# Linear attention ahead of two expert layers: the query exponential moved behind the transposes, the key maximum read from PSUM, zero-padded key tails, and the order of instructions from a table of offsets

## The chip, the cores and the metric

The kernel runs on one core of a Trainium2 chip. The time is device microseconds from the first to the last instruction of one launch, with what lies around them; smaller is better. The two versions are compared by the medians of several runs.

## What is computed

The program has three parts, one after the other: a linear attention, a mixture of eight experts, and a dense two-layer network with a rational activation. The change lies in the attention alone:

```
q_s = exp(q - max over d);   q_s = q_s / (sum over d + 1e-9)
k_s = exp(k - max over s);   k_s = k_s / (sum over s + 1e-9)
kv  = einsum('bhsd,bhse->bhde', k_s, v)
out = einsum('bhsd,bhde->bhse', q_s, kv)        # then laid out as 4608 rows of 512
```

There are 8 batches, 8 heads, 576 positions and a head size of 64, all in float32. The expert part then needs the router's logits of every row (and a skip score) before it knows which rows go to which expert.

## The kernel before

Each batch is cut into a main part of 512 positions (128 partitions times J = 4) and a tail of 64; the tails of two batches share one tile of 128 partitions. The function `attention` defines one small closure for each step and registers it with `op` under a name, an engine, a guessed duration, the steps it depends on and the buffers that it takes. For one batch the steps are these.

- Keys. `load_k` and `tail_k` bring the data in; `km2` and `km1` (L224, L231, L232) take maxima on VectorE; `krow` turns them with TensorE into PSUM (tile `pf`, L237), `kmx` (L247) reduces them, and `kbt` spreads the maximum over all partitions, again into `pf`. `kbc` (L256) is a ScalarE copy of this into the SBUF tile `kb`. `ksub0` on VectorE and `ksub2` on GpSimd (both L262) and `kst` (L268, the tail) subtract `kb`; `kexp0`, `kexp2` and `kxt` (L272, L276) are the exponentials on ScalarE. GpSimd sums them (`su2` L281, `su1` L286 and L287).
- Queries. `qx` (L293) is the maximum of each row on VectorE. With QA = 3, five heads are subtracted on GpSimd (`qs`, L303) and exponentiated in place (L313), and for three heads ScalarE does both at once with a bias (`qn` L297 negates the maximum, `qe` L310). The tail has `qxt`, `qst`, `qet` (L317, L321, L324). `tt` (L376) turns the exponentials with TensorE into PSUM (`pq`), and `tcp` (L380) copies them to SBUF as `eqT`.
- Products. `kv0` to `kv3` (L333, and L334 for the tail, which contracts the 64 partitions of its batch alone) accumulate k_s and v; `psum`, `rk` and `kn` (L339 to L349) normalise; `kvt`, `kvc`, `kvw`, `kwc` (L356 to L370) multiply the result with the router's weights; `tx` (L388) makes rows and logits at once. `tr`, `tl` (L394, L395, L413) and `tn` (L405 or L407) divide by the query's sum: `tn` is on VectorE except for the parts named in ON_ACT = (2,), which go to ScalarE. `store` sends 512 rows out, and `fin` (L428) adds up the logits.

PSUM has one `pf` bank for `krow`, `kbt` and `kvt` in turn, and one each for `pkv`, `psm` and `pq`; `px` has two buffers of two banks.

The order is made by `plan` (L136): it keeps a clock for each engine, takes the step that could start earliest, and among those within SLACK of it the one with the smallest due time, which is batch times PERIOD less a weighted length of the work behind the step. The steps are emitted in this order, and each engine, and SP's queue of transfers, runs its own steps strictly in it.

Of the kernel before, what the change touches and what calls it, by code (L numbers as in the profile page):

```python
# [37 lines left out]
QA = 3  # L38
URGENCY = {"pe": 2.16, "dve": 1.78, "act": 2.64, "pool": 1.71, "dma": 0.59}
HOP = 930.0  # L40
ROUND = 1.5 * 2 ** 23
TB = 384
PERIOD = 11200.0
SLACK = 100.0
ON_ACT = (2,)
# [90 lines left out]
def plan(ops, period, slack, sem=210.0, dma=1300.0):  # L136
    done, tail, users = {}, {}, {}
    for key, o in ops.items():
        for d in o["deps"]:
            users.setdefault(d, []).append(key)  # L140
    for key in reversed(list(ops)):
        tail[key] = ops[key]["dur"] * URGENCY[ops[key]["eng"]] + max([tail[u] + HOP for u in users.get(key, [])], default=0.0)
    prio = {key: o["batch"] * period - tail[key] for key, o in ops.items()}
    free, left, holds, order = {}, dict(ops), {}, []
    while left:
        cand = {}
        for key, o in left.items():
            if any(d in left for d in o["deps"]):
                continue
            wait = dma if o["eng"] == "dma" else sem  # L150
            t = max([done[d] + (wait if ops[d]["eng"] != o["eng"] else 0.0) for d in o["deps"]], default=0.0)
            for pool, bufs in o["takes"]:
                h = holds.get(pool, [])
                if len(h) >= bufs:
                    if any(u in left for u in h[-bufs]):
                        t = None
                        break
                    t = max([t] + [done[u] + wait for u in h[-bufs]])
            if t is not None:
                cand.setdefault(o["eng"], []).append((max(t, free.get(o["eng"], 0.0)), prio[key], key))  # L160
        eng = min(cand, key=lambda e: min(cand[e]))
        t0 = min(cand[eng])[0]
        t, _, key = min((c for c in cand[eng] if c[0] <= t0 + slack), key=lambda c: c[1])
        o = left.pop(key)
        free[eng] = t + o["dur"]
        done[key] = t + o["dur"] + o["lag"]
        for pool, _ in o["takes"]:
            holds.setdefault(pool, []).append(o["holds"][pool])
        order.append((t, key))
    return order, max(done.values())  # L170


def attention(tc, q, k, v, w_gate, w_skip, ca, cb, ident, ones, wg, av, bv, ab, logits, xd, gd, R):
    nc = tc.nc
    with ExitStack() as st:
# [38 lines left out]
        def load_tail(nm, bp):  # L214
            t = tails.tile([P, H, D], F32, name=nm + "t")
# [10 lines left out]
        def km1(b, c):  # L226
            m2, kt, hs = T["m2", b], T["kt", b // 2], part(b, c)[0]
# [24 lines left out]
        def kbc(b, c):  # L252
            hs, rs = part(b, c)
            if c == 0:
                T["kb", b] = work.tile([P, H, D], F32, name="kb", bufs=2)
# [18 lines left out]
        def kxt(b, c):  # L274
            kt = T["kt", b // 2][half(b), part(b, c)[0]]
# [7 lines left out]
        def su1(b):  # L283
            e2, kt = T["e2", b], T["kt", b // 2]
# [10 lines left out]
        def qn(b):  # L295
            T["qn", b] = work.tile([P, QA, J], F32, name="qn")
            nc.gpsimd.tensor_scalar(out=T["qn", b], in0=T["qx", b][:, H - QA:], scalar1=-1.0, scalar2=None, op0=ALU.mult)  # L297

        def qs(b):
            if ("eq", b) not in T:  # L300
                T["eq", b] = work.tile([P, J, H, D], F32, name="eq", bufs=3)
            hs = slice(0, H - QA)
            nc.gpsimd.tensor_tensor(out=T["eq", b][:, :, hs].rearrange("p j h d -> p h j d"), in0=T["q", b][:, hs],  # L303
                                    in1=T["qx", b][:, hs].unsqueeze(3).to_broadcast([P, H - QA, J, D]), op=ALU.subtract)

        def qe(b, j):
            if ("eq", b) not in T:
                T["eq", b] = work.tile([P, J, H, D], F32, name="eq", bufs=3)
            for h in range(H - QA, H):
                nc.scalar.activation(T["eq", b][:, j, h], T["q", b][:, h, j], AF.Exp, bias=T["qn", b][:, h - H + QA, j:j + 1])  # L310
            if QA < H:
                eq = T["eq", b][:, j, 0:H - QA]
                nc.scalar.activation(eq, eq, AF.Exp)  # L313
# [9 lines left out]
        def qet(b):  # L323
            nc.scalar.activation(T["qt", b // 2], T["qt", b // 2], AF.Exp)  # L324

        def kv(b, r):
# [3 lines left out]
            ek, vm, kt, vt, pkv = T["ek", b], T["v", b], T["kt", bp], T["vt", bp], T["pkv", b]  # L330
# [3 lines left out]
            nc.tensor.matmul(out=pkv[:, r, :], lhsT=kt[half(b), hs, :], rhs=vt[half(b), hs, :], start=False, stop=True)  # L334
# [95 lines left out]
        for b in range(B):  # L430
# [5 lines left out]
            k_users = {"k": fc("ksub0") + fc("ksub2"), "v": [("kv3", b)], "q": [("qe3", b)]}  # L436
            for nm in "kvq":
# [3 lines left out]
                if not odd:  # L441
                    tu = {"k": [("kv3", bo), ("su1", bo)], "v": [("kv3", bo)], "q": [("tt4", bo)]}[nm]
                    op("tail_" + nm, b, DMA, 1500.0, [], lambda nm=nm, b=b: load_tail(nm, b // 2), takes=[(nm + "t", 3, tu)], lag=900.0)
            for c in cs:
# [4 lines left out]
                for n, eng, dur, deps, fn, takes in (  # L449
                        ("km2", DVE, 1135.0, [d("load_k")], lambda b=b, c=c: km2(b, c), first(("m2", 1, fc("km1")))),  # L450
                        ("km1", DVE, 1331.0, [d("km2"), ("tail_k", be)], lambda b=b, c=c: km1(b, c), first(("m1", 1, fc("krow")))),
                        ("krow", PE, 440.0, [d("km1")], lambda b=b, c=c: krow(b, c), [("pf", 1, [d("kmx")])]),
                        ("kmx", DVE, 600.0, [d("krow")], lambda b=b, c=c: kmx(b, c), []),
                        ("kbt", PE, 440.0, [d("kmx")], lambda b=b, c=c: kbt(b, c), [("pf", 1, [d("kbc")])]),
                        ("kbc", ACT, 480.0, [d("kbt")], lambda b=b, c=c: kbc(b, c), first(("kb", 2, fc("ksub2") + fc("ksub0") + fc("kst")))),
                        ("ksub0", DVE, 1150.0, [d("kbc")], lambda b=b, c=c: ksub(b, c, nc.vector, 0), first(("ek", 2, [("kv3", b), ("su2", b)]))),
                        ("kst", DVE, 600.0, [d("kbc")], lambda b=b, c=c: kst(b, c), []),
                        ("ksub2", POOL, 2303.0, [d("kbc"), ("ksub0c0", b)], lambda b=b, c=c: ksub(b, c, nc.gpsimd, 2), []),
                        ("kexp0", ACT, 950.0, [d("ksub0")], lambda b=b, c=c: kexp(b, c, 0), []),
                        ("kexp2", ACT, 950.0, [d("ksub2")], lambda b=b, c=c: kexp(b, c, 2), []),  # L460
                        ("kxt", ACT, 520.0, [d("kst")], lambda b=b, c=c: kxt(b, c), [])):
                    op(f"{n}c{c}", b, eng, dur * w + 70.0 * (len(cs) - 1), deps + pc(n), fn, takes=takes)
            op("su2", b, POOL, 2303.0, fc("kexp0") + fc("kexp2"), lambda b=b: su2(b), takes=[("e2", 1, [("su1", b)])])
            op("su1", b, POOL, 2552.0, [("su2", b)] + fc("kxt"), lambda b=b: su1(b), takes=[("e1", 2, [("psum", b)])])
# [766 lines left out]
```

## Time and profile before

| | us |
|---|---|
| median of 3 runs | 1425.42 |
| lowest and highest | 1420.71, 1426.38 |
| the profiled execution | 1417.86 |
| its span | 1416.2 |

In the views below a name such as L262 is a line of the kernel, `out<-in` are the program's tiles, a shape is partitions x elements, and an engine's "idle before" is put down to what ended it. PE is TensorE, DVE is VectorE, ACT is ScalarE, POOL is GpSimd, SPq is the queue that issues transfers.

### The profile page before, as it was taken

Reading aid. Unit: us, or ns where it says so; the run is one execution under the profiler, and the core shown is the slowest. Engines: PE = TensorE matmul, PEld = TensorE weight load, DVE = VectorE, ACT = ScalarE, POOL = GpSimd, SP = SyncE. Lnnn points to the kernel's source line nnn. Section 1 sums busy time; section 2 is a strip of 40 time slices with the busy share of each in tenths; the row PEclk is TensorE's granted clock in tenths of the full one; section 3 lists DMA queues with packets and bytes.
Section 4 is the critical chain, followed back from the end, with each engine's and each line's share of the span. In section 5 each row is a group of like instructions: output and inputs, shape, how many; then the busy total and the mean of one; then the engine's idle time right before and its main releaser. Section 6 shows DMA issues by size and latency. Waiting matters only on the chain.

```text
span 1416.2 us, 22263 instructions
## 1 busy us (share of the span) xinstructions
PE 1338.9 (95%) x7470; PEld 1206.2 (85%) x7470; DVE 1129.7 (80%) x2091; ACT 919.4 (65%) x1811; POOL 314.6 (22%) x252
## 2 busy tenths in 40 slices
PE   5888949999899999799999999999999999999998
PEld 4877939888789889688999999999999999999997
DVE  7799775657665655499988888888888888888887
ACT  2756713635342422499887878787778787878776
POOL 6655414556445443143000000000000000000000
PEclk9999969999999999899999999999999999999999
DMA  9885365566646574331010100000000000000000
GB/s 279 212 260 166 106 176 172 209 241 214 225 157 235 199 259 163 115 133 57 23 45 1 45 23 23 23 23 23 23 23 23 23 23 23 23 23 23 1 23 23
DMA packets 86928, 143.82 MB, mean 102 GB/s; under 512 B 21924, under 2 KB 52644, under 8 KB 85744
## 3 DMA queue, kind: packets, MB, share of 16 engines
q1 hardware_dynamic: 79696, 125.88, 27.1%
q0 software_dynamic: 7072, 16.06, 3.7%
q8 instruction: 70, 1.15, 0.3%
q14 instruction: 90, 0.74, 0.2%
HBM read 110.66 MB, written 35.15 MB: 103 GB/s over the span
## 4 chain that ended last, share of the span: by engine, by line
PE 54%; ACT 2%; DVE 2%; DMA 0%; issue 0%; ACTq 0%; SPq 0%
PE py L1168 26%; PE ph L1123 26%; PE pt L1107 1%; DVE gl L1149 0%; DMA wos<-wc_out 0%; DVE qq L1147 0%; ACT gh L1132 0%; ACT qq L1138 0%; DVE pn L1155 0%; ACT m L1136 0%; ACT pn L1140 0%; DVE qq L1153 0%; ACT r L1143 0%; DVE r L1151 0%; DVE pn L1157 0%
## 5 line engine op out<-in xcount | busy, mean ns | idle before, releaser
L1168 PE MATMUL py<-woh,gl 128*128 128x512 f32 x576 | 227.5, 395 | 0.2 <-DVE gl L1149 0.2
L1168 PE MATMUL py<-woh,gh 128*128 128x512 f32 x576 | 227.4, 395 | 0.0
L1168 PE MATMUL py<-wol,gh 128*128 128x512 f32 x576 | 226.9, 394 | 0.0
L1132 ACT CAST gh<-pn 128x384 fp32r<-128x384 f32 x192 | 98.8, 514 | 142.2 <-PE py L1168 137.0
L1149 DVE TENSOR_TENSOR gl<-pn,gh 128x384 fp32r<-128x384 f32 x192 | 110.0, 573 | 69.5 <-ACT gh L1132 69.5
L1138 ACT ACTIVATE qq<-m,ab 128x384 f32<-128x384 f32 x192 | 136.5, 711 | 6.4
L1123 PE MATMUL ph<-xh,wi0h 128*128 128x384 f32 x384 | 129.6, 338 | 0.3 <-DVE pn L1158 0.2
L1123 PE MATMUL ph<-xh,wi0l 128*128 128x384 f32 x384 | 129.6, 338 | 0.0
L1123 PE MATMUL ph<-xl,wi0h 128*128 128x384 f32 x384 | 129.0, 336 | 0.0
L1168 PEld LDWEIGHTS py<-woh,gl 128*128 128x128 f32 x576 | 108.0, 188 | 24.4 <-DVE gl L1149 1.2
L1140 ACT ACTIVATE pn<-ph,av 128x384 f32<-128x384 f32 x192 | 125.7, 655 | 0.0
L1158 DVE SCALAR_TENSOR_TENSOR pn<-pn,av,ph 128x384 f32<-128x384 f32 x192 | 118.1, 615 | 6.8
L1168 PEld LDWEIGHTS py<-wol,gh 128*128 128x128 f32 x576 | 108.2, 188 | 17.8
L1168 PEld LDWEIGHTS py<-woh,gh 128*128 128x128 f32 x576 | 108.3, 188 | 17.4 <-ACT gh L1132 0.5
L1153 DVE TENSOR_TENSOR qq<-m,qq 128x384 f32<-128x384 f32 x192 | 106.9, 557 | 17.9 <-ACT qq L1138 4.3
L830 PE MATMUL ph<-xth,w1h 128*128 128x256 f32 x416 | 119.1, 286 | 1.6 <-ACT cvs L760 0.7
L830 PE MATMUL ph<-xtl,w1h 128*128 128x256 f32 x416 | 118.8, 286 | 0.1
L830 PE MATMUL ph<-xth,w1l 128*128 128x256 f32 x416 | 118.6, 285 | 0.0
L1155 DVE SCALAR_TENSOR_TENSOR pn<-pn,av,r 128x384 f32<-128x384 f32 x192 | 117.4, 611 | 0.1
L1143 ACT ACTIVATE r<-qq,qc 128x384 f32<-128x384 f32 x192 | 116.0, 604 | 0.0
L1147 DVE SCALAR_TENSOR_TENSOR qq<-qq,r 128x384 f32<-128x384 f32 x192 | 108.7, 566 | 0.0
L1151 DVE SCALAR_TENSOR_TENSOR r<-qq,r 128x384 f32<-128x384 f32 x192 | 106.9, 557 | 0.0
(236 smaller groups left out, 3331.0 us busy)
## 6 DMA issues: line engine op xcount, KB each, us to landing
hold<-in_moe_w_dram SPq DMA_DIRECT2D x8, 2048.0 KB, 9.2
w2s<-in_moe_w_dram SPq DMA_DIRECT2D x8, 2048.0 KB, 10.1
hold<-xd SPq DMA_DIRECT2D x12, 768.0 KB, 4.3
out_dram<-o SPq DMA_DIRECT2D x36, 256.0 KB, 2.1
vm<-in_v_dram SPq DMA_DIRECT2D x8, 1024.0 KB, 9.3
qm<-in_q_dram SPq DMA_DIRECT2D x8, 1024.0 KB, 10.6
xd<-xs SPq DMA_DIRECT2D x8, 1024.0 KB, 5.3
raw<-in_moe_w_in_dram SPq DMA_DIRECT2D x16, 512.0 KB, 7.9
```

The lines of the kernel that those rows point to most:

```text
L830: nc.tensor.matmul(out=ph[:, u, :], lhsT=a[:, k, fs], rhs=b[:, k, :], start=(n == 0), stop=(n == 3 * KD - 1))
L1123: nc.tensor.matmul(out=ph, lhsT=w[:, k, :], rhs=x[:, k, :], start=(n == 0), stop=(n == 3 * KD - 1))
L1138: nc.scalar.activation(qq, m, AF.Identity, scale=ab[:, 1:2], bias=ab[:, 0:1])
L1140: nc.scalar.activation(pn, ph, AF.Identity, scale=av[:, 3:4], bias=av[:, 2:3])
L1143: nc.scalar.activation(r2, T[("q",) + second], AF.Ln, bias=qc)
L1147: nc.vector.scalar_tensor_tensor(out=q3, in0=q3, scalar=1.0 + 1e-6, in1=r3, op0=ALU.add, op1=ALU.mult)
L1149: GL(nc).tensor_tensor(out=gl, in0=pn4, in1=gh.bitcast(F32), op=ALU.subtract)
L1151: nc.vector.scalar_tensor_tensor(out=r3, in0=q3, scalar=2.0, in1=r3, op0=ALU.subtract, op1=ALU.mult, reverse0=True)
L1153: nc.vector.tensor_tensor(out=qq, in0=m, in1=qq, op=ALU.mult)
L1155: nc.vector.scalar_tensor_tensor(out=p3, in0=p3, scalar=av[:, 0:1], in1=r3, op0=ALU.add, op1=ALU.mult)
L1158: nc.vector.scalar_tensor_tensor(out=pn, in0=pn, scalar=av[:, 1:2], in1=ph, op0=ALU.add, op1=ALU.mult)
L1168: nc.tensor.matmul(out=py, lhsT=g[:, ts_], rhs=w[:, f, :], start=(f == 0 and n == 0), stop=(f == KF - 1 and n == 2))
```

## The change

- `tcp` becomes an exponential that reads PSUM; the transposes turn the differences q - max. `qn`, `qe`, `qet` go, and `qs` subtracts all eight heads on GpSimd, in two instructions of four heads.
- `kbc` and the tile `kb` go. `ksub0`, `ksub2` and `kst` read the spread maximum straight from `pf`; `ksub2` moves from GpSimd to VectorE. The bank stays taken until all three are done.
- The key tails lie in four fixed tiles, each with 64 partitions zeroed once by GpSimd at the start, and the tail's product contracts all 128 partitions. There are two pairs of tail buffers in place of three.
- `tn0` goes to ScalarE beside `tn2` (not for the last batch, as before).
- `plan` is replaced: every step has a moment, batch times PERIOD + OFFSET of its name + SHIFT of its batch, and the steps are emitted in the order of these moments, each as soon as what it depends on, and the users of the buffer that it takes, have been emitted.

```diff
-QA = 3
-PERIOD = 11200.0
-ON_ACT = (2,)
+PERIOD = 16040
+SHIFT = [-160, -440, -700, -1800, -2750, -2900, -3460, -4400]
+OFFSET = {
...
+    "kexp2c1": -23420, "qx1": -22210, "kstc0": -19620, "tail_v": -18620, "tx2": -18400, "su1": -15680, "km2": -14420, "load_v": -13390,
...
+ON_ACT = (0, 2)
...
+def plan(ops):
+    def at(key):
...
+        return b * PERIOD + OFFSET[name] + SHIFT[b]
...
+    while left:
+        key = next(k for k in left if ready(k))
...
+        for i in range(NKT):
+            t = keep.tile([P, H, D], F32, name=f"kt{i}")
+            nc.gpsimd.memset(t[64 * (1 - i % 2):64 * (1 - i % 2) + 64], 0.0)
...
-            nc.scalar.copy(T["kb", b][:, hs], T["pb", b, c][:, rs].rearrange("p r (h d) -> p (r h) d", h=2))
...
-                              in1=T["kb", b][:, hs].unsqueeze(2).to_broadcast([P, hs.stop - hs.start, 2, D]), op=ALU.subtract)
+                                    in1=kb(b, c).unsqueeze(2).to_broadcast([P, hs.stop - hs.start, 2, D]), op=ALU.subtract)
...
-            nc.tensor.matmul(out=pkv[:, r, :], lhsT=kt[half(b), hs, :], rhs=vt[half(b), hs, :], start=False, stop=True)
+            nc.tensor.matmul(out=pkv[:, r, :], lhsT=kt[:, hs, :], rhs=vt[:, hs, :], start=False, stop=True)
...
-            nc.scalar.copy(T["eqT", b, j], T["pq", b, j])
+            nc.scalar.activation(T["eqT", b, j], T["pq", b, j], AF.Exp)
...
-                        ("kbt", PE, 440.0, [d("kmx")], lambda b=b, c=c: kbt(b, c), [("pf", 1, [d("kbc")])]),
+                        ("kbt", PE, 440.0, [d("kmx")], lambda b=b, c=c: kbt(b, c), [("pf", 1, [d("ksub2"), d("kst")])]),
...
-                        ("ksub2", POOL, 2303.0, [d("kbc"), ("ksub0c0", b)], lambda b=b, c=c: ksub(b, c, nc.gpsimd, 2), []),
+                        ("ksub2", DVE, 1180.0, [d("kbt"), ("ksub0c0", b)], lambda b=b, c=c: ksub(b, c, 2), []),
```

Sorted by this table, GpSimd's queue repeats su2, su1, (qst,) qs0, qs1 of one batch. VectorE's queue, from the second half of the keys of batch 4 on, reads: ksub2.4 kn.3 km1.5 tr1.2 tl1.2 tn1.2 tr2.2 tl2.2 kmx.5 qx0.4 qx1.4 tr3.2 tl3.2 tn3.2 fin.2 ksub0.5 kst.5 tr0.3 tl0.3 rk.4 km2.6, then the tables, then ksub2.5 and so on (the number is the batch). SP's queue in the middle reads: load_k.5 store.0 tail_v.4 load_v.4 load_q.4 load_k.6 store.1 tail_q.4 store_tail.1 tail_k.6 load_v.5 load_q.5 load_k.7 store.2.

## Rows read from the trace of the kernel before

**Rows 1.** Stretch, length, busy PE, PEld, DVE, ACT, POOL, clock, DMA share, GB/s.

```profile
0.00:35.00 35.00, 18.34 (x68) 14.16 (x68) 26.89 (x30) 10.53 (x21) 22.61 (x30) 1.00 1.03 279
35.00:70.00 35.00, 31.75 (x220) 28.41 (x220) 27.66 (x43) 24.68 (x69) 23.82 (x14) 1.00 0.79 210
70.00:105.00 35.00, 28.09 (x212) 25.78 (x213) 34.20 (x57) 21.93 (x64) 20.79 (x27) 0.96 0.89 256
105.00:140.00 35.00, 29.97 (x209) 27.25 (x208) 34.15 (x68) 20.56 (x54) 20.60 (x11) 0.89 0.59 168
140.00:181.00 41.00, 37.82 (x305) 35.27 (x302) 32.32 (x94) 27.45 (x84) 14.29 (x14) 1.00 0.43 118
```

**Rows 2.** Timeline of VectorE at the end of the attention: start, us, instruction.

```profile
180.09 0.78 DVE L428 TENSOR_REDUCE logits<-lr 128x45 f32<-128x360 f32 x1
```

**Rows 3.** Timeline of SP's queue behind it.

```profile
191.15 2.13 SPq L787 DMA_DIRECT2D hold<-in_moe_w_dram  x4
```

**Rows 4.** VectorE's waits in the attention: us in total, times, longest.

```profile
DVE rq L394 <- PE px L388: 7.3, 10, 1.7
DVE m L224 <- DMA km<-in_k_dram: 5.6, 2, 4.1
```

**Rows 5.** VectorE's groups with each shape apart: busy us, mean ns.

```profile
L262 DVE TENSOR_TENSOR ek<-km,kb 128x1024 f32<-128x1024 f32 x7 | 15.4, 2193 | 1.9 <-ACT kb L256 1.9
L231 DVE TENSOR_TENSOR m<-m 128x512 f32<-128x512 f32 x7 | 13.7, 1962 | 0.1
L224 DVE TENSOR_TENSOR m<-km 128x1024 f32<-128x1024 f32 x7 | 11.9, 1693 | 0.1
L268 DVE TENSOR_TENSOR kt<-kt,kb 64x512 f32<-64x512 f32 x7 | 11.1, 1579 | 0.2
L232 DVE TENSOR_TENSOR m<-m,kt 64x512 f32<-64x512 f32 x7 | 9.9, 1412 | 0.2
L268 DVE TENSOR_TENSOR kt<-kt,kb 64x256 f32<-64x256 f32 x2 | 2.7, 1341 | 0.0
```

**Rows 6.** Single lines: duration in ns, least, median and most.

```profile
L293 DVE TENSOR_REDUCE qx<-qm x16: 1202/1208/1220, 19.9 to 152.6; 128x16 f32<-128x1024 f32 x16
L407 DVE TENSOR_TENSOR xs<-px,rq x25: 639/679/682, 53.3 to 177.7; 128x512 f32<-128x512 f32 x25
```

**Rows 7.** Timeline of all engines from 95 us on, VectorE and GpSimd alone.

```profile
95.09 5.95 DVE L231 TENSOR_TENSOR m<-m 128x512 f32<-128x512 f32 x1
...
95.66 2.33 POOL L303 TENSOR_TENSOR eq<-qm,qx 128x1280 f32<-128x1280 f32 x1
...
98.16 2.34 POOL L262 TENSOR_TENSOR ek<-km,kb 128x1024 f32<-128x1024 f32 x1
```

**Rows 8.** ScalarE's groups with each shape apart: busy us, mean ns, idle before.

```profile
L310 ACT ACTIVATE eq<-qm,qn 128x64 f32<-128x64 f32 x96 | 26.2, 338 | 2.2 <-POOL qn L297 2.1
L380 ACT COPY eqT<-pq 128x512 f32<-128x512 f32 x36 | 21.1, 586 | 22.3 <-PE pq L376 19.5 <-PE px L388 2.6
L313 ACT ACTIVATE eq<-eq 128x320 f32<-128x320 f32 x32 | 14.6, 457 | 0.0
L405 ACT ACTIVATE xs<-px,rq 128x64 f32<-128x64 f32 x56 | 12.3, 334 | 2.0 <-DVE lr L413 1.4 <-issue 0.5
L324 ACT ACTIVATE qt<-qt 128x512 f32<-128x512 f32 x4 | 2.5, 623 | 0.4 <-POOL qt L321 0.4
```

**Rows 9.** Timeline of TensorE around one tail product.

```profile
74.31 1.06 PE L333 MATMUL pkv<-vm,ek 128*128 128x128 f32 x8
75.29 0.49 PE L334 MATMUL pkv<-vt,kt 64*128 64x128 f32 x2
75.71 0.66 PE L237 MATMUL pf<-ident,m 128*128 128x128 f32 x4
```

**Rows 10.** Timeline of GpSimd: its first tensor operation.

```profile
10.60 1.71 POOL L262 TENSOR_TENSOR ek<-km,kb 128x512 f32<-128x512 f32 x1 [5.87 <-ACT kb L256]
```

**Rows 11.** The waits of SP's queue: us in total, times, longest.

```profile
SPq L417 <- DVE xs L407: 67.6, 6, 20.2
```

More of the change, by code (lines that the diff above doesn't have):

```diff
@@ L133, in tail_col @@
     return bp * (2 * J + 1) + 2 * J
[L136 to L144, printed above, removed]
-    while left:
[L146 to L170, printed above, removed]
@@ new lines, in plan, with ready @@
+def plan(ops):
+    def at(key):
+        name, b = key
+        if b and name.endswith("c0"):
+            name = name[:-2]
+        return b * PERIOD + OFFSET[name] + SHIFT[b]
+    left, holds, order = sorted(ops, key=at), {}, []
+    gone = set()
+    def ready(key):
+        o = ops[key]
+        if any(d not in gone for d in o["deps"]):
+            return False
+        return all(len(holds.get(p, [])) < n or all(u in gone for u in holds[p][-n]) for p, n in o["takes"])
+    while left:
+        key = next(k for k in left if ready(k))
+        left.remove(key)
+        gone.add(key)
+        for p, _ in ops[key]["takes"]:
+            holds.setdefault(p, []).append(ops[key]["holds"][p])
+        order.append(key)
+    return order
@@ L214, in load_tail @@
         def load_tail(nm, bp):
+            if nm == "k":
+                for i in range(2):
+                    b = 2 * bp + i
+                    nc.sync.dma_start(out=kts[b % NKT][64 * i:64 * i + 64], in_=k[b, :, MAIN:S, :].rearrange("h p d -> p h d"))
+                return
             t = tails.tile([P, H, D], F32, name=nm + "t")
@@ L250, in kbt, with kb, ksub @@
             T["pb", b, c] = rows(lambda r: T["mx", b][:, r:r + 1].to_broadcast([P, P]), part(b, c)[1])
[L252 to L255, printed above, removed]
-            nc.scalar.copy(T["kb", b][:, hs], T["pb", b, c][:, rs].rearrange("p r (h d) -> p (r h) d", h=2))
-        def ksub(b, c, eng, j0):
+        def kb(b, c):
+            return T["pb", b, c][:, part(b, c)[1]].rearrange("p r (h d) -> p (r h) d", h=2)
+        def ksub(b, c, j0):
             hs = part(b, c)[0]
@@ L274, in kxt @@
         def kxt(b, c):
-            kt = T["kt", b // 2][half(b), part(b, c)[0]]
+            kt = kts[b % NKT][half(b), part(b, c)[0]]
             nc.scalar.activation(kt, kt, AF.Exp)
@@ L293, in qx, with qs @@
             nc.vector.tensor_reduce(out=T["qx", b][:, hs], in_=T["q", b][:, hs], op=ALU.max, axis=AX.X)
[L295 to L313, printed above, removed]
+        def qs(b, h):
+            if h == 0:
+                T["qd", b] = work.tile([P, J, H, D], F32, name="qd", bufs=3)
+            hs = slice(4 * h, 4 * h + 4)
+            nc.gpsimd.tensor_tensor(out=T["qd", b][:, :, hs].rearrange("p j h d -> p h j d"), in0=T["q", b][:, hs],
+                                    in1=T["qx", b][:, hs].unsqueeze(3).to_broadcast([P, 4, J, D]), op=ALU.subtract)
         def qxt(b):
@@ L435, in attention @@
             fc = lambda n: [(f"{n}c{c}", b) for c in cs]
-            k_users = {"k": fc("ksub0") + fc("ksub2"), "v": [("kv3", b)], "q": [("qe3", b)]}
+            k_users = {"k": fc("ksub0") + fc("ksub2"), "v": [("kv3", b)], "q": [("qs1", b)]}
             for nm in "kvq":
@@ L449, in attention @@
                 for n, eng, dur, deps, fn, takes in (
-                        ("km2", DVE, 1135.0, [d("load_k")], lambda b=b, c=c: km2(b, c), first(("m2", 1, fc("km1")))),
-                        ("km1", DVE, 1331.0, [d("km2"), ("tail_k", be)], lambda b=b, c=c: km1(b, c), first(("m1", 1, fc("krow")))),
+                        ("km2", DVE, 1250.0, [d("load_k")], lambda b=b, c=c: km2(b, c), first(("m2", 1, fc("km1")))),
+                        ("km1", DVE, 1400.0, [d("km2"), ("tail_k", be)], lambda b=b, c=c: km1(b, c), first(("m1", 1, fc("krow")))),
@@ L457, in attention @@
[L457 to L461 removed]
+                        ("kmx", DVE, 700.0, [d("krow")], lambda b=b, c=c: kmx(b, c), []),
@@ new lines, in attention @@
+                        ("kbt", PE, 440.0, [d("kmx")], lambda b=b, c=c: kbt(b, c), [("pf", 1, [d("ksub2"), d("kst")])]),
+                        ("ksub0", DVE, 1180.0, [d("kbt")], lambda b=b, c=c: ksub(b, c, 0), first(("ek", 2, [("kv3", b), ("su2", b)]))),
+                        ("kst", DVE, 690.0, [d("kbt")], lambda b=b, c=c: kst(b, c), []),
+                        ("ksub2", DVE, 1180.0, [d("kbt"), ("ksub0c0", b)], lambda b=b, c=c: ksub(b, c, 2), []),
+                        ("kexp0", ACT, 1060.0, [d("ksub0")], lambda b=b, c=c: kexp(b, c, 0), []),
@@ L462, in attention @@
+                        ("kexp2", ACT, 1060.0, [d("ksub2")], lambda b=b, c=c: kexp(b, c, 2), []),
+                        ("kxt", ACT, 620.0, [d("kst")], lambda b=b, c=c: kxt(b, c), [])):
                     op(f"{n}c{c}", b, eng, dur * w + 70.0 * (len(cs) - 1), deps + pc(n), fn, takes=takes)
[L463 to L464 removed]
+            op("su2", b, POOL, 2400.0, fc("kexp0") + fc("kexp2"), lambda b=b: su2(b), takes=[("e2", 1, [("su1", b)])])
@@ L472, in attention @@
-            for j in range(J):
-                op(f"qe{j}", b, ACT, 240.0 * QA + (90.0 + 53.3 * (H - QA)) * (QA < H), [("qn", b), ("qs", b)] + [(f"qe{j - 1}", b)] * (j > 0), lambda b=b, j=j: qe(b, j),
-                   takes=eq_take if QA == H and j == 0 else [])
+                op(f"qx{h}", b, DVE, 1180.0, [("load_q", b)] + [("qx0", b)] * h, lambda b=b, h=h: qx(b, h), takes=[("qx", 2, [("qs1", b)])] if h == 0 else [])
+                op(f"qs{h}", b, POOL, 2130.0, [(f"qx{h}", b)] + [("qs0", b)] * h, lambda b=b, h=h: qs(b, h), takes=[("qd", 3, [("tt3", b)])] if h == 0 else [])
@@ L488, in attention @@
-            op("kwc", b, ACT, 180.0, [("kvw", b)], lambda b=b: kwc(b))
+            op("kvc", b, ACT, 600.0, [("kvt", b)], lambda b=b: kvc(b), takes=[("kvT", 1, [("kvw", b)])])
+            op("kvw", b, PE, 900.0, [("kvc", b)], lambda b=b: kvw(b), takes=[("psm", 1, [("kwc", b)])])
+            op("kwc", b, ACT, 370.0, [("kvw", b)], lambda b=b: kwc(b))
             for j in range(nj):
-                src = ("qet", b) if j == J else (f"qe{j}", b)
+                src = ("qst", b) if j == J else ("qs1", b)
@@ L496, in attention @@
-                op(f"tl{j}", b, DVE, 145.0, [(f"tr{j}", b)] + chain("tl"), lambda b=b, j=j: tl(b, j), takes=[("lr", 2, [("fin", b)])] if j == 0 else [])
-                op(f"tn{j}", b, ACT if j in ON_ACT and b < B - 1 else DVE, 1590.0 if j in ON_ACT and b < B - 1 else 605.0, [(f"tl{j}", b)] + chain("tn"), lambda b=b, j=j: tn(b, j),
+                op(f"tr{j}", b, DVE, 350.0, [(f"tx{j}", b)] + chain("tr"), lambda b=b, j=j: tr(b, j), takes=[("rq", 2, [(f"tn{i}", b) for i in range(nj)])] if j == 0 else [])
@@ L498, in attention @@
+                op(f"tl{j}", b, DVE, 220.0, [(f"tr{j}", b)] + chain("tl"), lambda b=b, j=j: tl(b, j), takes=[("lr", 2, [("fin", b)])] if j == 0 else [])
+                op(f"tn{j}", b, ACT if j in ON_ACT and b < B - 1 else DVE, 2650.0 if j in ON_ACT and b < B - 1 else 670.0, [(f"tl{j}", b)] + chain("tn"), lambda b=b, j=j: tn(b, j),
                    takes=[("xs", 2, [("store", b)])] if j == 0 else [("xt", 2, [("store_tail", b)])] if j == J else [])
@@ L518, in load_small @@
             nc.sync.dma_start(out=bv, in_=cb.unsqueeze(0).to_broadcast([P, 2]))
-        order, span = plan(ops, PERIOD, SLACK)
+        order = plan(ops)
         with tc.manual_schedule():
-            for _, key in order:
+            for key in order:
                 ops[key]["fn"]()
```

57 lines of the change are left out of this document (22 added, 35 removed), and 11 rows, old and new, of the table OFFSET.

## The prediction

> **What bounds the kernel now.** The chain of waits is of no help here: followed back from the end it stays in the last part of the program. So I read the stretches first. The attention ends at 180.87 us, where `fin` of the last batch has the last logits [rows 2]; the first expert weights are fetched 10 us later, because their number comes out of these logits [rows 3]. Nothing of the experts can begin before, so what the attention saves comes off the whole time one for one, and nothing else in the program is changed. In the table by stretch VectorE is the fullest engine: 34.20 and 34.15 of 35 us between 70 and 140, and 26.89 + 27.66 + 34.20 + 34.15 + 32.32 = 155.2 us of the 181 in all; ScalarE and GpSimd have room everywhere, and TensorE is full in the last stretch alone [rows 1]. VectorE's 25.8 idle us are mostly waits at the start, for the first keys (5.6), and for `tx` (7.3) [rows 4]. So the first question is what VectorE's 155.2 us consist of.
>
> Its groups answer that. A subtraction of 1024 elements takes 2.19 us, a maximum of 512 takes 1.96, a subtraction of 512 takes 1.58 [rows 5], yet a maximum over 1024 never takes more than 1.22 and a product of 512 that reads PSUM never more than 0.682 [rows 6]. The stretched ones all read two SBUF tiles. One of them shows how: L231 begins at 95.09 and ends at 101.04, and GpSimd runs two tensor operations in that time, the last of them done at 100.50 [rows 7]. While GpSimd works, a VectorE instruction with two SBUF operands stands still, and all of its queue with it; one with one SBUF operand, or with PSUM, does not.
>
> **The change part by part**, on VectorE first. Undisturbed prices are 1.21 us for 1024 elements and 0.68 for 512 [rows 6], half as much for half (0.6 and 0.4, my estimate).
>
> - `ksub0` and `kst` read their maximum from PSUM, so each keeps one SBUF operand and should no longer be held. `ksub0`: 15.4 - 7 x 1.21 = 6.9 us less. `kst`: 11.1 + 2.7 - 7 x 0.68 - 2 x 0.4 = 8.2 us less [rows 5]. Together 15.1. No row has a subtraction of an SBUF tile and a PSUM tile of this size; the nearest is L407, which reads PSUM beside SBUF and shows no hold in 25 cases, so I take all of it; the other bound is none of it.
> - `ksub2` comes from GpSimd: 7 x 1.21 + 2 x 0.68 = 9.8 us more.
> - `tn0` leaves for seven batches: 7 x 0.68 = 4.8 us less. On ScalarE it is eight instructions of 0.334 us each, 12.3 us for the seven if they cost what `tn2` costs [rows 8].
> - `km2` and `km1` keep two SBUF operands. Their holds are now 11.9 - 8.5 + 13.7 - 4.8 + 9.9 - 4.8 = 17.4 us [rows 5]. What becomes of them is a matter of the order. In the table's queue `km1` stands two places behind `ksub2`; GpSimd's next step, `su2`, needs the exponential of what `ksub2` just made, so GpSimd should be idle then. `km2` stands behind all of qx, tn3, fin, ksub0 and kst, when the train su2, su1, qs0, qs1 should be nearly through. I take two thirds as gone, 11.6 us; the bounds are all of it, and none.
> - Idle time stays at 25.8 us. New waits of VectorE for `kbt` and old ones for `tx` may trade places; I allow 8 us either way, which is about the whole of the second [rows 4].
>
> TensorE: 32 tail products contract 128 partitions. Before, a pair of tail instructions took 75.71 - 75.29 = 0.42 us from start to start, a pair of full ones 0.98 / 4 = 0.245 [rows 9]; 32 x 0.175 = 5.6 us less, worth nothing by itself while VectorE sets the pace. The zeroing is four small fills on GpSimd, whose first real work came only at 10.60 [rows 10], and now comes later still.
>
> ScalarE loses L310 and L313 (26.2 + 14.6 us), the copies `kbc` and the tail's exponential (2.5), and gains the 12.3 of `tn0`. An exponential of 128x512 takes 623 ns against 586 for the copy that it replaces [rows 8]: 36 x 0.04 = 1.3 us, hidden. ScalarE had more than 10 us of room in every stretch [rows 1], so none of that counts in the sum; it shortens the path from `qx` to `tx`, and that is why I let the idle time not grow.
>
> GpSimd loses `ksub2` and `qn` and gains three heads: 2.33 us for five [rows 7] makes 3.7 for eight. It ends below its 102 us [rows 1].
>
> Transfers: their number and size stay. In SP's queue each store now stands in front of the next loads of values and queries, and waits for `tn2` on ScalarE; the queue already spent 67.6 us behind stores without starving VectorE beyond the start [rows 4, 11]. With two pairs of key tails instead of three, `tail_k` waits for a batch further back; it is asked for more than a batch ahead, so I cost it at nothing. If the cover is gone, a late key load costs up to the longest such wait, 20.2 us, once.
>
> [...]
>
> **The sum.** 155.2 - 15.1 + 9.8 - 4.8 - 11.6 = 133.5 us busy, plus 25.8 idle, makes an attention of 159.3 us in place of 180.9: 21.6 us less. The profiled execution took 1417.9 us (span 1416.2), so 1396.3 on its own scale. The median of the three runs stands 7.6 us above it; from 1425.4 the sum gives **1403.8**, and that is what I predict. The bounds: holds all gone and 8 us less idle give 35 us less, 1390; holds as before and 8 us more idle give 2 less, 1423.
>
> **The rivals.** *Another floor is met first.* TensorE's 146.0 us less 5.6, plus its empty 16.7 us at the start, is 157; the transfers of the first four stretches, 32.0 MB at the first stretch's 279 GB/s, need 115 us, and 41 behind them make 156 [rows 1]. All stand within 3 us of my 159, so a loss of some per cent on either decides: at 250 GB/s the transfers end at 169, 12 us saved, 1413. For it: three nearly full resources in one queue order. [...]
>
> *The time goes into waits.* Every engine must keep the table's order; the old planner balanced guessed clocks, the table just sorts. If VectorE's idle time grows by the 20 us that its busy time falls, the attention takes 179 and the time is 1424. For it: `krow` of the next batch stands behind `kv0`, which needs an exponential of the keys that were just subtracted. Against: ScalarE's load is almost halved.
>
> *The bank is held (slower).* `pf` is taken from `kbt` until the third subtraction, and `km2` stands between them in VectorE's queue. `kvt`, `kvc` and the next `krow` want the same bank. If GpSimd's train is not through at that place, `km2` waits as L231 did, 5.95 - 0.68 = 5.3 us [rows 7], now with the bank locked, and TensorE's next products queue behind it. Seven batches would cost 37 us: 159 + 37 = 196, so 15 us slower, 1441. It decides from 3.1 us a batch on (21.6 / 7). For it: GpSimd's train has four tensor operations in a row, as in rows 7. Against: all copies of `kb` through ScalarE fall away, and the place was worked out above. [...] No row of before has a bank read by three instructions in turn.
>
> *The holds do not end.* If one SBUF operand in a strided view is held too, 15.1 us return and `ksub2` adds holds of its own: with the 0.98 us mean of `ksub0`'s, 9 more. Then 159 + 24 = 183, 1427, no gain. L293 speaks against it: 16 cases without a hold [rows 6].
>
> **How the numbers follow.** My forecast, with some 8 to 35 us saved, has 0.60. The floors have 0.17, still faster by about 12. Waits have 0.10 and holds that stay 0.04: within 0.5%, which is 7 us and about what a measurement of this kernel can tell from no change. The held bank has 0.09. Faster is 0.60 + 0.17 = 0.77, the same 0.14, slower 0.09. The range reaches from the bound at 1390 to the floors' 1413 and on towards the waits, to 1421.
>
> **What would show it.** In the changed profile L262 and L268 should have means of 1.2 and 0.7 us with a longest not far above; all 18 subtractions of the main keys should be on VectorE; the holds of the three maxima should add up to about 6 us; the last `fin` should end near 159; VectorE's idle time should be near 26. I am wrong if VectorE's waits for `pf` exceed some 8 us in total, if `km2` shows durations of several us, or if the attention ends after 174.

## The result, and the profile after

The changed kernel takes 1397.8 us (median of 4 runs, 1395.0 to 1400.4) against 1423.1 beside it: a ratio of 0.9832, 95% interval 0.9806 to 0.9859. The profiled execution took 1394.98 us (span 1393.3), 22.9 us less than the one of before. The forecast of 1403.8 was 6 us too high, inside its range, with the right sign. Of these 6 us, 1.3 lie between the profiled executions (22.9 us saved, 21.6 forecast); the other 4.7 come from the medians, which stood 7.6 us above the profiled execution when the forecast was made and stand 2.8 above it here.

The stretches of the changed kernel, with the columns of [rows 1]:

```profile
0.00:35.00 35.00, 15.33 (x89) 13.15 (x90) 23.37 (x33) 7.63 (x11) 18.80 (x31) 0.95 1.08 279
35.00:70.00 35.00, 34.22 (x296) 33.27 (x295) 33.93 (x70) 21.65 (x59) 26.58 (x31) 1.00 1.09 321
70.00:105.00 35.00, 31.53 (x259) 30.41 (x260) 33.52 (x84) 20.64 (x57) 19.23 (x12) 0.95 0.86 273
105.00:140.00 35.00, 34.25 (x294) 33.38 (x293) 29.22 (x75) 21.28 (x65) 21.11 (x17) 1.00 0.43 143
140.00:153.00 13.00, 9.79 (x81) 8.86 (x79) 9.26 (x30) 4.58 (x15) 0.00 (x0) 1.00 0.25 84
```

VectorE's timeline at the end of the attention (compare [rows 2]):

```profile
152.10 0.78 DVE L420 TENSOR_REDUCE logits<-lr 128x45 f32<-128x360 f32 x1
```

The attention ends at 152.88 in place of 180.87: 28.0 us earlier, 6.4 more than forecast. Up to there VectorE is busy for 129.2 us (155.1 before; forecast 133.5) and idle for 23.7 (25.8). TensorE is now as full as VectorE: 34.22 and 34.25 of 35 us in two stretches. Where VectorE's time went, by group (compare [rows 5]):

```profile
L270 DVE TENSOR_TENSOR ek<-km,pf 128x1024 f32<-128x1024 f32 x14 | 16.9, 1208 | 0.0
...
L235 DVE TENSOR_TENSOR m<-km 128x1024 f32<-128x1024 f32 x7 | 10.5, 1500 | 0.6 <-DMA km<-in_k_dram 0.6
L243 DVE TENSOR_TENSOR m<-m,kt 64x512 f32<-64x512 f32 x7 | 8.9, 1270 | 0.2
...
L242 DVE TENSOR_TENSOR m<-m 128x512 f32<-128x512 f32 x7 | 4.8, 686 | 0.1
L276 DVE TENSOR_TENSOR kt<-kt,pf 64x512 f32<-64x512 f32 x7 | 4.8, 684 | 0.1
...
L270 DVE TENSOR_TENSOR ek<-km,pf 128x512 f32<-128x512 f32 x4 | 2.6, 677 | 0.0
```

The subtractions have no hold left: 1208 and 684 ns, where the prediction wrote 1.21 and 0.68. The three maxima keep 10.5 - 8.5 + 8.9 - 4.8 = 6.1 us of holds; the longest single `km2` (L235) takes 2.84 us. One hold in the timeline, of `km1` beside `su2`: VectorE's L243 ends 0.55 us behind GpSimd's L289.

```profile
91.63 2.54 POOL L289 TENSOR_TENSOR e<-ek 128x1024 f32<-128x1024 f32 x1 [7.05 <-ACT ek L280]
...
91.99 2.73 DVE L243 TENSOR_TENSOR m<-m,kt 64x512 f32<-64x512 f32 x1
```

Of the 28.0 us, 5.1 are given back behind the attention in this pair of executions. The queue of transfers there, and the waits of VectorE and of that queue (us in total, times, longest):

```profile
150.07 1.11 SPq L610 DMA_DIRECT2D gd<-r_gate  x2
153.46 0.34 SPq L409 DMA_DIRECT2D xd<-xs  x1
154.28 1.84 SPq L414 DMA_DIRECT2D xd<-xt  x2
165.36 2.12 SPq L770 DMA_DIRECT2D hold<-in_moe_w_dram  x4
```
```profile
DVE rq L386 <- PE px L380: 6.6, 8, 2.2
...
DVE mx L258 <- PE pf L248: 3.3, 3, 1.6
DVE lh L707 <- DMA xd<-xt: 2.1, 1, 2.1
DVE kt L276 <- PE pf L248: 1.6, 2, 0.8
```
```profile
SPq L409 <- DMA gd<-r_gate: 2.2, 1, 2.2
```

The table puts the stores of the gate's values in front of the last stores of rows. So the last tail leaves 1.4 us behind the last `fin`, the token table (L707) waits for it, and the first expert weights are fetched 12.5 us behind the attention, where it was 10.3 [rows 2, 3]. In the kernel of before the gate's stores stand in front as well, but they were issued 9 us before the attention's end, and the last tail left ahead of it:

```profile
170.89 1.12 SPq L627 DMA_DIRECT2D gd<-r_gate  x2
...
180.20 1.10 SPq L422 DMA_DIRECT2D xd<-xt  x2
```

These 2.2 us are less than half of the 5.1; the rest comes behind the first weights, and its cause is not shown.

### The profile page after: what moved, and what is told of

The parts are those of the page before. It is cut to its first block, busy times and chain, and to the rows that moved or that the text cites. A ratio compares the mean times of both kernels' runs of the same rounds, so it can differ in the third digit from the quotient of the medians.

```text
span 1393.3 us, 22173 instructions
## 1 busy us (share of the span) xinstructions
PE 1320.0 (95%) x7470; PEld 1195.8 (86%) x7470; DVE 1099.6 (79%) x2093; ACT 890.4 (64%) x1726; POOL 296.5 (21%) x247
## 4 chain that ended last, share of the span: by engine, by line
PE 55%; DVE 2%; issue 1%; ACT 1%; DMA 1%; POOL 0%; POOLq 0%; ACTq 0%; DVEq 0%
PE ph L1106 27%; PE py L1151 27%; DMA xd<-y,sidx 1%; PE pt L1090 1%; DVE gl L1132 0%; DVE qq L1130 0%; DVE r L1134 0%; DVE qq L1136 0%; DVE pn L1140 0%; DVE pn L1138 0%; ACT qq L1121 0%; ACT m L1119 0%; DVE pn L1141 0%; POOL x L792 0%; ACT gh L1115 0%
## 5 line engine op out<-in xcount | busy, mean ns | idle before, releaser
L1106 PE MATMUL ph<-xh,wi0h 128*128 128x384 f32 x384 | 129.6, 338 | 0.3 <-DVE pn L1141 0.2
L1106 PE MATMUL ph<-xh,wi0l 128*128 128x384 f32 x384 | 129.7, 338 | 0.0
L1106 PE MATMUL ph<-xl,wi0h 128*128 128x384 f32 x384 | 129.0, 336 | 0.0
L1151 PEld LDWEIGHTS py<-woh,gl 128*128 128x128 f32 x576 | 108.0, 188 | 24.4 <-DVE gl L1132 1.2
```

The source lines that it names most:

```text
L1106: nc.tensor.matmul(out=ph, lhsT=w[:, k, :], rhs=x[:, k, :], start=(n == 0), stop=(n == 3 * KD - 1))
L1151: nc.tensor.matmul(out=py, lhsT=g[:, ts_], rhs=w[:, f, :], start=(f == 0 and n == 0), stop=(f == KF - 1 and n == 2))
```

## The experiments

All ratios are to the kernel of before, on the same chip. "Attention", "busy" and "idle" (VectorE's, up to the attention's end) are from one profiled execution each; two executions of the changed kernel itself ended the attention at 152.9 and 156.9, so where these are closer than some 4 us the ratio decides. "Median" is in us; the kernel of before had medians from 1421.2 to 1423.1 on the chips used.

| kernel | median | ratio, 95% interval | attention | busy | idle |
|---|---|---|---|---|---|
| before | 1421 to 1423 | 1 | 180.9 | 155.1 | 25.8 |
| changed | 1397.8 | 0.9832 (0.9806 to 0.9859) | 152.9 | 129.2 | 23.7 |
| e12_after_again | 1397.8 | 0.9847 (0.9809 to 0.9884) | 156.9 | 129.6 | 27.3 |
| e1_kb_sbuf | 1423.7 | 1.0030 (1.0011 to 1.0050) | 174.1 | 141.9 | 32.2 |
| e9_kb_psum_copy | 1416.8 | 0.9961 (0.9938 to 0.9984) | 174.7 | 129.9 | 44.7 |
| e13_copy_tails3 | 1414.8 | 0.9942 (0.9919 to 0.9965) | 171.1 | 130.0 | 41.1 |
| e2_qexp_first | 1403.8 | 0.9876 (0.9843 to 0.9908) | 161.8 | 129.7 | 32.1 |
| e3_tail64 | 1406.3 | 0.9899 (0.9865 to 0.9932) | 162.3 | 129.0 | 33.3 |
| e5_tn0_dve | 1404.8 | 0.9873 (0.9831 to 0.9915) | 156.0 | 132.9 | 23.0 |
| e4_old_planner | 1411.9 | 0.9924 (0.9894 to 0.9953) | 168.0 | 135.8 | 32.1 |
| e8_psum_only | 1418.9 | 0.9965 (0.9945 to 0.9986) | 176.3 | 141.8 | 34.5 |
| e10_before_pad | 1415.7 | 0.9957 (0.9937 to 0.9976) | 176.8 | 154.4 | 22.4 |
| e6_gate_late | 1391.5 | 0.9796 (0.9763 to 0.9830) | 153.8 | 129.4 | 24.4 |
| e11_gate_tn4 | 1411.2 | 0.9938 (0.9913 to 0.9963) | 171.3 | 128.0 | 43.3 |

### The place of the key maximum

```diff
-            return T["pb", b, c][:, part(b, c)[1]].rearrange("p r (h d) -> p (r h) d", h=2)
+            return T["kb", b][:, part(b, c)[0]]
...
+            nc.scalar.copy(T["kb", b][:, hs], T["pb", b, c][:, rs].rearrange("p r (h d) -> p (r h) d", h=2))
...
```

> The changed kernel, but ScalarE copies the key maximum out of PSUM again and the three subtractions (all still on VectorE) read the copy, so that each has two SBUF operands. Theory (a VectorE instruction with two SBUF operands stands still while GpSimd works): the subtractions are held as before, 6.9 us for ksub0 and 8.2 us for kst, and ksub2 on VectorE as ksub0, 6.9 us more; together up to 22 us, means of 2.2 and 1.6 us instead of 1.21 and 0.68, and about 1415 to 1420 us. Rival (the order of the table keeps VectorE and GpSimd apart, the operand's place matters little): means stay near 1.2 and 0.7 us, the seven copies of 0.6 us and their hops add at most some 5 us, 1398 to 1403.

The whole gain is gone: 1423.7 is above what either side expected, though the holds are smaller than expected. VectorE's groups of e1 show the holds back:

```profile
L276 DVE TENSOR_TENSOR ek<-km,kb 128x1024 f32<-128x1024 f32 x14 | 22.9, 1638 | 2.6 <-ACT kb L270 2.5
...
L282 DVE TENSOR_TENSOR kt<-kt,kb 64x512 f32<-64x512 f32 x7 | 9.2, 1307 | 0.1
...
L276 DVE TENSOR_TENSOR ek<-km,kb 128x512 f32<-128x512 f32 x4 | 2.5, 676 | 0.0
```

They cost 22.9 - 16.9 + 9.2 - 4.8 = 10.4 us of the 12.7 that VectorE is busier. That would be my theory, were it not for the control, in which the copy goes from the PSUM tile onto itself:

```diff
+            return T["pb", b, c][:, part(b, c)[1]].rearrange("p r (h d) -> p (r h) d", h=2)
...
+            nc.scalar.copy(kb(b, c), kb(b, c))
...
```

> The control of e1_kb_sbuf: ScalarE makes the same copy at the same place in its queue, but from the PSUM tile onto itself, so that the subtractions wait for the copy as there and still read PSUM. Theory (in e1_kb_sbuf it was the second SBUF operand that cost the time): the subtractions stay at 1.21 and 0.68 us, VectorE's busy time stays near 129 us, and what is left is the hop over ScalarE: the attention ends between 154 and 162 us instead of 174.1, about 1400 to 1408. Rival (in e1_kb_sbuf it was the copy and its hop, with the order broken by them): the attention ends at 170 us or later, 1417 to 1424.

The rival won. The subtractions run at 1208 and 683 ns, busy time is 129.9, and the attention still ends at 174.7. Comparing the two ratios, the holds cost about 0.7% (10 us); the copy in ScalarE's queue costs more, 1.3% (18 us), though e9 also keeps the bank longer than e1. (That the two profiled executions end alike, 174.1 and 174.7, says little: e1's was the fastest of its ten runs, e9's the second slowest.) Both prices hold for the copy where these runs put it, right behind `kbt`, in a table made without it; no table made with the copy was run. Waits of e9 in its first 72 us, ScalarE's and the transfer queue's:

```profile
ACT pf L267 <- PE pf L248: 26.0, 5, 8.7
```
```profile
SPq L224 <- PE pkv L329: 14.6, 1, 14.6
```

The copy for the next batch stands in ScalarE's queue ahead of exponentials of this one, and holds them back until its maximum is there. The products of batch 1 come late, and the third tail load, which needs a buffer that they free, blocks all loads for 14.6 us. The last run, e9 with a third pair of key tails, asks which of the two carries it:

```diff
-        NKT = 4
+        NKT = 6
```

> e9_kb_psum_copy with buffers for three pairs of key tails instead of two. There the attention lost 21.8 us without any hold of the subtractions; in its first 70 us SP's queue stood 14.6 us behind the third tail load, which waits for the last product of batch 1 to free its buffer, and ScalarE's queue stood 26.0 us in front of the copies. If the tail load carries the loss: its wait goes, the attention ends between 158 and 163 us, 1401 to 1407. If the copies in ScalarE's queue carry it (the late products of batch 1 are their consequence, and the load only follows): the wait at the load goes too, but ScalarE still waits over 20 us for pf and the attention ends at 170 us or later, 1413 to 1418.

```profile
ACT pf L267 <- PE pf L248: 24.2, 5, 8.1
```

The load's wait is gone, ScalarE's is not, and the ratio's interval overlaps that of e9: the copies carry most of it, if not all. In the changed kernel itself the two pairs of tails show no cost: its queue has no wait at a key tail load. Three pairs were not run there.

### One part alone, in the kernel of before

```diff
-            nc.scalar.copy(T["kb", b][:, hs], T["pb", b, c][:, rs].rearrange("p r (h d) -> p (r h) d", h=2))
...
-            nc.vector.tensor_tensor(out=kt, in0=kt, in1=T["kb", b][half(b), hs], op=ALU.subtract)
+            nc.vector.tensor_tensor(out=kt, in0=kt, in1=kb(b, c)[half(b)], op=ALU.subtract)
...
```

> The kernel of before with its planner, with one part of the change alone: the key maximum is read from PSUM, no copy of it is made, and ksub2 is on VectorE. Theory: ksub0 and kst lose their holds, 15.1 us, ksub2 adds 9.8 on VectorE, so VectorE's busy time falls by 5.3 us, GpSimd has 16 us less, which also takes some holds from km2 and km1: 5 to 12 us less than before, 1411 to 1418. Rival (a held bank): the pf bank is taken until the third subtraction, VectorE's and TensorE's waits for pf grow by more than 5 us, 1423 or more.

The 1418.9 lies between the two. VectorE is 13.3 us less busy, but the attention is only 4.6 us shorter. The difference is in VectorE's waits:

```profile
DVE rq L391 <- PE px L385: 11.7, 17, 2.7
DVE ek L259 <- PE pf L237: 7.1, 4, 3.7
...
DVE mx L247 <- PE pf L237: 3.4, 3, 2.4
```

Waits for `pf` are 10.5 us, where the same view of before has 0.7, and 2.4 for the copy `kb`:

```profile
DVE ek L262 <- ACT kb L256: 2.4, 2, 1.9
...
DVE mx L247 <- PE pf L237: 0.7, 2, 0.5
```

That the bank is what holds things up shows on TensorE: by the profile its `krow` waits for `kst` to give the bank back, a wait that before does not have:

```profile
PE pf L237 <- DVE kt L265: 7.3, 3, 2.9
```

So the held bank is real in e8. In the table's order VectorE's waits for `pf` are 3.3 + 1.6 = 4.9; under the old planner with all the other parts of the change (e4, below) they are 5.0 + 0.7 = 5.7.

```diff
-            nc.tensor.matmul(out=pkv[:, r, :], lhsT=kt[half(b), hs, :], rhs=vt[half(b), hs, :], start=False, stop=True)
+            nc.tensor.matmul(out=pkv[:, r, :], lhsT=kt[:, hs, :], rhs=vt[:, hs, :], start=False, stop=True)
...
```

> The kernel of before with one part of the change alone: zero-padded key tails, so that the 32 tail products contract 128 partitions. Measured by e3_tail64 a pair of 64-row instructions costs TensorE 0.28 us more than a pair of 128-row ones (0.10 at its start, 0.18 behind it), 9 us in all. Theory of the prediction (nothing while VectorE's queue sets the pace): within 3 us of before, 1418 to 1424. Rival (TensorE's time is on the path in before too, where VectorE waits 7.3 us for px): 5 to 9 us less than before, 1412 to 1416.

About 6 us, so the padding (with the two pairs of buffers that belong to it) is worth something even where VectorE is busy for 34 of 35 us: VectorE's busy time is the same, and its idle time falls by 3.4.

### One part undone, in the changed kernel

```diff
-            nc.tensor.matmul(out=pkv[:, r, :], lhsT=kt[:, hs, :], rhs=vt[:, hs, :], start=False, stop=True)
+            nc.tensor.matmul(out=pkv[:, r, :], lhsT=kt[half(b), hs, :], rhs=vt[half(b), hs, :], start=False, stop=True)
```

> The changed kernel, but each of the 32 tail products of the keys contracts the 64 partitions of its own batch instead of all 128 (the zeros stay, unread). TensorE gets about 32 x 0.175 = 5.6 us more. Theory (VectorE bounds, TensorE's part is worth nothing by itself): no more than 2 us, 1396 to 1400. Rival (TensorE, 34.2 of 35 us busy in two of the stretches, is the bound now): most of the 5.6 us come back, 1402 to 1404.

The attention is 9.4 us longer, more than either theory had. TensorE's timeline, of the changed kernel and then of e3:

```profile
75.38 1.13 PE L325 MATMUL pkv<-vm,ek 128*128 128x128 f32 x8
76.35 0.39 PE L326 MATMUL pkv<-vt,kt 128*128 128x128 f32 x2
76.57 0.60 PE L248 MATMUL pf<-ident,m 128*128 128x128 f32 x4
```
```profile
73.63 1.14 PE L325 MATMUL pkv<-vm,ek 128*128 128x128 f32 x8
74.70 0.48 PE L326 MATMUL pkv<-vt,kt 64*128 64x128 f32 x2
75.11 1.16 PE L325 MATMUL pkv<-vm,ek 128*128 128x128 f32 x8
```

A pair of 64 rows delays its own start (1.07 against 0.97) and what follows (0.41 against 0.22): 0.29 us, and 32 x 0.29 = 9.3. Within the spread of 4 us the whole of it reaches the attention's end, and the ratio agrees (0.67%, 9.5 us). TensorE has no room there:

```profile
35.00:70.00 35.00, 34.95 (x271) 32.11 (x272) 31.94 (x62) 19.68 (x56) 23.89 (x30) 0.99 1.08 322
...
105.00:140.00 35.00, 34.99 (x279) 32.03 (x278) 26.46 (x61) 19.59 (x56) 17.89 (x12) 1.00 0.48 164
```

```diff
+            nc.scalar.activation(qd, qd, AF.Exp)
...
-            nc.scalar.activation(T["eqT", b, j], T["pq", b, j], AF.Exp)
+            nc.scalar.copy(T["eqT", b, j], T["pq", b, j])
...
```

> The changed kernel, but the query exponential stands in front of the transposes again, in place, as one ScalarE instruction for each of the 36 blocks, and the eviction behind the transposes is a plain copy. It adds about 36 x 0.62 = 22 us to ScalarE and removes some 1.3. Theory (VectorE bounds the attention, ScalarE has 13 us of room in each 35): the attention ends within 3 us of 152.9, 1396 to 1401. Rival (the freed ScalarE is where the 6.4 us come from by which the forecast was short): VectorE's waits for tx grow, the attention ends near 160 or later, 1404 to 1415.

ScalarE is 17.2 us busier (93.0 against 75.8), still little more than half of the time, and the attention is 8.9 us longer. VectorE's wait for `px` doubles:

```profile
DVE rq L390 <- PE px L384: 12.5, 10, 4.9
```

The interval of the ratio overlaps that of the changed kernel; it is this wait that speaks for a real loss, since it stayed at 6.6 us in the slower execution of the changed kernel too (e12).

```diff
-ON_ACT = (0, 2)
+ON_ACT = (2,)
```

> The changed kernel, but tn0 is on VectorE again in all batches (tn2 stays on ScalarE). VectorE gets 7 x 0.68 = 4.8 us more, ScalarE 7 x about 2.6 less. Theory (VectorE's busy time is the bound one for one): the attention ends 3 to 5 us later, 1401 to 1403. Rival (VectorE has slack now, another engine sets the pace): under 1.5 us, 1397 to 1399, and waits on VectorE shrink by what it adds.

The attention is 3.1 us longer for 3.7 more busy. That is as the theory has it, but less than the spread of 4 us, and the interval of the ratio overlaps that of the changed kernel, so this run leaves the price of `tn0` open. Behind the attention the first weights are fetched 15.7 us later, in place of 12.5; the changed kernel itself has 16.4 in e12.

### The order alone

The `plan` of before, with its old constants (PERIOD 11200), on the changed kernel's operations:

> The changed kernel's operations, put in order by the planner of before with its old constants instead of the table. Theory of the prediction (busy time of VectorE is the bound; the holds of the subtractions end by their operand, those of km2 and km1 by the order): the subtractions stay at 1.2 and 0.7 us, km2 and km1 are held up to 17 us again instead of 6, and waits may grow; the attention ends near 165, about 1408 to 1412. Rival A (the order brings nothing of its own): within 2 us of 1397.8. Rival B (the operations bring nothing without the order; waits replace the busy time): 1418 or more.

As forecast by the prediction's theory, to the upper end: the attention takes 15.1 us more, 6.6 of it busy time (the three maxima are held for 10 us, L241 at 1164 ns) and the rest waits, above all for `px`:

```profile
DVE rq L385 <- PE px L379: 13.7, 13, 2.5
```

### Behind the attention

```diff
-    "gate_out": -190950, "tl2": -184420, "kexp0c0": -139510, "tt2": -129050, "load_kc0": -101540, "kbtc0": -94130, "kv3": -90430, "krow": -83430,
+    "gate_out": 390950, "tl2": -184420, "kexp0c0": -139510, "tt2": -129050, "load_kc0": -101540, "kbtc0": -94130, "kv3": -90430, "krow": -83430,
```

> The changed kernel, but the stores of the gate's values stand at the end of SP's queue, behind the last stores of the attention, instead of in front of them. Theory (part of the gain of 28.0 us is given back behind the attention, because the last tail store waits in SP's queue behind the gate's stores and the token table on VectorE waits 2.1 us for it): store_tail is issued within 1 us of the last tn, the token table waits under 0.5 us, and 1.5 to 3 us come off, 1395 to 1396. Rival (what follows the token table waits for something else anyway, the transposes or the weights): the wait goes, and the time stays within 0.7 us of 1397.8.

```profile
153.13 1.11 SPq L414 DMA_DIRECT2D xd<-xt  x2
154.29 0.58 SPq L608 DMA_DIRECT2D gd<-r_gate  x1
...
164.07 2.11 SPq L770 DMA_DIRECT2D hold<-in_moe_w_dram  x4
```

The weights are fetched 10.3 us behind the attention again, as before, and what is behind the attention takes 1235.4 us, as before (1235.3; 1240.4 in the changed kernel). All four runs (1390.8 to 1394.0) are below all ten of the changed kernel (1395.0 to 1409.2). It is the fastest version found, and the gain of 6 us is more than the theory's 1.5 to 3.

The runs show the gain; how it comes about the profiles do not settle. The time behind the attention lies between 1235 and 1252 us in the executions profiled here, 1244.4 in e10, whose gate's stores stand as in before, with the first weights at 10.3. And e11 below, with the gate's stores as late as here, has the wait of 2.1 us and the 12.5 all the same. So the exact return to 1235.4 is in part luck, and the place of the gate's stores is the likely cause of the loss, not a shown one.

> The changed kernel itself, once more beside e11_gate_tn4 on one chip. Expected 1396 to 1399. If the gate's stores cost what e6_gate_late showed, e11_gate_tn4 stands 4 to 8 us below it; if e6_gate_late was only a better sample, less than 2 us.

Six runs, four of them from 1395 to 1398 and two at 1409, one of these profiled. There the first stretch moved 256 GB/s in place of 279, the attention ended 4 us later, and the last tail, issued 1.9 us behind the last `fin`, was waited for longer:

```profile
DVE lh L707 <- DMA xd<-xt: 6.0, 1, 6.0
```

Why it then loses 6 us more behind the first weights stays open. Whether the gate's stores explain e6, as this run was to ask beside e11, stays open with it, since e11 missed for another reason.

```diff
-ON_ACT = (0, 2)
+ON_ACT = (0, 2, 4)
```

> The gate's stores behind the last stores, as in e6_gate_late, and besides tn4 of batches 1, 3 and 5 on ScalarE. VectorE gets 3 x 0.68 = 2.0 us less, ScalarE 24 instructions of about 0.33 us more. If VectorE still sets the pace, 1389 to 1390; if TensorE does now (34.2 of 35 us in two stretches), or if px is held longer by the slower reader, 1391 to 1395.

A miss by 16 us: 1411. VectorE is 1.4 us less busy than in e6 and idle for 19 more. ScalarE stands before `tn4` until VectorE has the sums, the next batch's exponentials stand behind it, and TensorE waits for those. Three rows of waits, of ScalarE, TensorE and VectorE:

```profile
ACT xt L397 <- DVE lr L405: 10.7, 2, 6.0
```
```profile
PE pq L368 <- ACT eqT L372: 10.4, 5, 3.2
```
```profile
DVE rq L386 <- PE px L380: 19.9, 12, 4.7
```

## Why the prediction was right, and where it was not

- **`ksub0` and `kst` lose their holds, `ksub2` costs 9.8.** Right, and shown twice: 1208 and 684 ns here, 1638 and 1307 with the copy in SBUF. The rival that holds stay is out.
- **The holds of `km2` and `km1` go by two thirds.** Right: 6.1 us are left of 17.4. The reason was half right. In e8, with the old planner, about 9.7 are left, so most went with that part of the change alone, probably because GpSimd lost `ksub2`; the order gave the rest. And 4.1 of the 6.1 are on `km1`, for which GpSimd "should be idle": in the case shown `su2` runs beside it.
- **VectorE's sum.** 4.3 us too high. It left out holds in the tables: their four stretched groups took 7.4 us before and take 2.5 now, none of them held.
- **Idle time stays.** Right as a number (23.7), wrong as a reason. It stays because other parts of the change worked for it: undone one at a time, the padding, the exponential and the order bring 8 to 10 us of idle time each, the copy 21 (one execution each; the changed kernel's second had 3.6 more itself).
- **Padding worth nothing, ScalarE's work hidden.** Both steps failed. The padding is worth 9.4 us here, about 6 in before; the exponential's place about 6 to 9. A mean share of busy time, or a full VectorE, was taken for cover. TensorE's term was also mis-sized: 0.175 us a pair counted only the delay behind the pair [rows 9], the runs showed 0.29.
- **The copy `kbc` costed at nothing.** This failed most: put back into the table's order it costs about 18 us by itself, more than the holds that it causes, since ScalarE's queue stood in front of these copies (26.0 us in e9's first 72, what stands behind them held back with them). What it cost in the kernel of before, where the planner had chosen its place, no run shows.
- **The floor of TensorE, 157.** Not met, but near. TensorE needed 125.1 us, not 140, and with its 19.7 empty us at the start the floor lies at 145. Why it needed so much less is only in part shown: the tail pairs gave more than costed, but the mean granted clock of the attention went from 0.97 to 0.98 only. The rival's mechanism is what e3 shows.
- **The held bank.** It exists (10.5 us in e8). That the table's order is what avoids it does not follow, since e4 without the table has 5.7. Even in e8 the ratio is below 1 (0.9965); in the table's order the cost is 4.9 us and the gain far larger. The reading from PSUM itself showed no price: four unheld subtractions of 128x512 take 677 ns in the mean with a PSUM operand and 676 without (e1).
- **What came after.** The prediction took what the attention saves as saved one for one. 5.1 of 28.0 came back in the profiled execution, 2.2 of them ahead of the first weights; e6 makes the place of the gate's stores the likely cause. The 6.4 us by which the attention did better and these 5.1 nearly cancel, and that is luck: the 1403.8 is nearer than its reasons deserve.

The parts don't add up: undone one by one in the changed kernel they cost some 28 (the copy with its holds), 13 (the order), 10 (the padding), 6 (the exponential) and 6 us (`tn0`), the last two within the noise of the ratios; together far more than the 24 won. The likely reason is that each removes a limit that would else have bound.

## What to carry to other kernels

Where engines are within some per cent of each other in a fixed order, as TensorE and VectorE are here (34.22 and 33.93 of 35 us in one stretch), "hidden" is not a price: time taken off an engine that is full in a stretch counted (9.3 us of TensorE's, 9.4 of the attention's), and so did a step taken out of a chain between engines (the copy, about 18 us). Price a copy by what stands behind it in its queue, not by its own 0.57 us (e9); and when steps move to another engine, choose their places in its order anew. Look also at what the transfer queue has in front of the last transfer that someone waits for (2.2 us for the gate's stores here).

## What was not expected of the hardware

In e8 more is held beside GpSimd than VectorE instructions with two SBUF operands: a cast of 128x3 elements, with one SBUF operand, takes 3.40 us where it takes 0.17 in the kernels of before and after, and ends at 96.36 with GpSimd's train (96.33):

```profile
92.78 1.26 POOL L284 TENSOR_TENSOR e<-e,kt 64x512 f32<-64x512 f32 x1
...
92.96 3.40 DVE L573 CAST r_pf<-r_pidx 128x3 f32<-128x3 int32 x1
...
94.00 2.33 POOL L300 TENSOR_TENSOR eq<-qm,qx 128x1280 f32<-128x1280 f32 x1
```

The hold spans two GpSimd instructions in a row. So the prediction's rule, that an instruction with one SBUF operand does not stand still, is too wide; its evidence was a reduction [rows 6], and reductions stayed free in the changed kernel too (sixteen of 1024 elements, 1.21 us in the mean).

And a TensorE pair that contracts 64 partitions is dearer than one that contracts 128 with zeros, by 0.29 us in the pair shown, in a stretch with a granted clock of 0.95 in both kernels. The larger part of it, the delay of what follows, is nearly the same in the other pairs: all six of e3 between 74 and 92 us have the next start after 0.41 or 0.42 us, as have 24 of the 29 of before with no wait behind them; of such pairs in the changed kernel 28 of 29 have it after 0.22 or 0.23.
